# Fewer unread products ahead of the first real ones, and an earlier read of the last flag

## The chip, the cores and the metric

The kernel runs on one core of one Trainium2 chip. The metric is the device time of one execution in microseconds, as the median of several timed executions. Before the change it is 584.61 us (three executions, 584.51 to 585.43). A profiled execution is slower by what the profiler adds and is shown beside it.

## The reference

Two blocks follow one another. The first is a gated linear attention over 4 batches, 8 heads, 768 tokens and heads of 48; the second is a bilinear feed-forward over the 3072 resulting tokens with a model width of 384 and an inner width of 1536. All values are float32.

```python
def _attn_ref(q, k, v, f_logit):
    f = 1.0 / (1.0 + np.exp(-f_logit))
    state = np.zeros((B, H, D, D), dtype=np.float32)
    for t in range(S):
        state = f[:, :, t, :, None] * state + np.einsum('bhd,bhe->bhde', k[:, :, t], v[:, :, t])
        y[:, :, t] = np.einsum('bhd,bhde->bhe', q[:, :, t], state)
    return y

def _moe_ref(x, w_a, w_b, w_out):
    return (x @ w_a) * (x @ w_b) @ w_out
```

## The kernel before, in words

The program is one long straight line, with an order written by hand at the front, an order made by a planner behind it, and a branch at the end.

The attention is cut into 16 units: a unit is one batch, one half of the tokens (384) and four heads. For each unit the gates are turned into running products along the tokens; k is multiplied by the inverse products and q by the products, both on VectorE (line 374). After that the unit is plain matrix work on TensorE (PE): `turn` (line 455) transposes k, ScalarE copies it out (`turned`, line 462), `scores` (line 426) makes the 64 x 64 blocks of q times k, VectorE masks them (line 443), `gains` (line 506) makes each block's addition to the state, VectorE sums these (`carried`, lines 535 and 537), `within` (line 566) multiplies the masked scores by v and `across` (line 592) adds the part that comes from the state. ScalarE copies the unit's output from PSUM (`out_of_bank`, line 610) and DMAs store it into the tile `xT` (line 632), where the feed-forward reads it. The DMAs of the first two units are spread over the queues of SP, ScalarE and GpSimd, and all weight loads are issued on SP's queue, in program order between the other DMAs.

The feed-forward works on blocks of 384 tokens. Block 0 and 1 use plain products (`up`, line 676), the later blocks a scheme with fewer products and more sums (`up_triples`, line 803), and `down_thirds` (line 1010) does the same for the second matrix. The weights are converted in pieces on ScalarE, GpSimd and VectorE (lines 71 to 83, started by `begin` and finished by `end`).

At the front nothing of the feed-forward can run yet: the gates of units 0 and 1 must be turned into products, and the first weights loaded and converted. PE would stand idle. There the kernel issues matrix products whose result nobody reads, with `keep_up(n, width, rows)` (line 1195): the identity times some columns of the gate products, into a PSUM bank that is overwritten later. Before the change there are 17 of 128 columns ahead of `turn(0)`, 10 of 128 columns behind `gains(0)`, and 47 on 64 rows and 64 columns behind these, ahead of `turn(1)`; three more of 384 columns stand between the output of unit 1 and the first `up`, and stay. A float32 product is two matmul instructions on PE, each with its own weight load, so the profile counts it twice. Which engine does what is written down in program order, and each engine runs its own instructions in that order.

At the end the last block's `down_thirds(blk, ending)` makes, in this order, the products v1, u1, v2, r2, u2, v3, r3, u3, v4, t1, u4, v5, t2, u5, v6, each of four float32 products (eight matmul instructions). From them three row groups of the output are summed in the tile `w_ba`: row group 0 out of u3, t1, u4, v4, v5 and t2, group 1 out of u1, r2 and others, with its left half finished by v6 alone, and group 2 out of v1, v2, r3, u5 and others. The method assumes that the gates do not decay too far. A flag `bad` tells whether they did: VectorE sums what was noted on the way (`sum_held`), PE adds that over the partitions (line 1153), VectorE compares it (line 1154), and `read_bad` (line 1159) loads the flag into a register of every engine's sequencer. Then every engine branches (line 142): with the flag set, the whole output is computed again by another method; otherwise the last sums and stores run, which are kept in the list `ending`, and the program is over. In the input at hand the flag is not set.

Of the kernel before, what the change touches and what calls it, by code (L numbers as in the profile page):

```python
# [109 lines left out]
def kernel(  # L110
# [29 lines left out]
    with ExitStack() as pools:  # L140
        again, ending = by_quotients(pools, tc, q, k, f_logit, v, moe_w_a, moe_w_b, moe_w_out, out, ident, weights, bad, banks)
# [12 lines left out]
def by_quotients(ctx, tc, q, k, f_logit, v, moe_w_a, moe_w_b, moe_w_out, out, ident, weights, bad, ps_f):  # L154
    nc = tc.nc
    B, H, D, S = q.shape
    w_ba, w_out = weights
# [120 lines left out]
    def begin(n):  # L278

        while 2 * n > begun[0] < 2 * len(todo):  # L280
            i, second = divmod(begun[0], 2)
            dst, src, shape = todo[i]
            if not second:
                going.append(
                    from_double(
                        nc, dst, raws[i], shape[0], next(blocks), bits[i % len(bits)], some, whole, shape[0] == NKT
                    )
                    if src.dtype != FP32 else iter(())
                )
            next(going[i], None)  # L290
            begun[0] += 1
# [18 lines left out]
    PE, DVE, ACT, POOL, SP = range(5)  # L310
# [135 lines left out]
    def turn(u):  # L446

        kf = halves(sets[u % NSET]["k"])
        live.setdefault(u, {})["kT"] = sb1.tile([128, 2, NC, R + D], FP32, tag="kT", name="kT")
        ps = live[u]["turned"] = [ps_f[idle.pop(0)] for _ in range(2)] if u in FIRST else pair_of(away(u))  # L450
        used = ident[0:R + D, 0:R + D]
        for n in range(2):
            for c in range(NC):
                o = n * BLK + c * C
                nc.tensor.transpose(ps[n][:, c * (R + D):(c + 1) * (R + D)], kf[0:R + D, o:o + C], used)
# [37 lines left out]
    def gains(u, chunks=range(NC), halves=range(2)):  # L493

        _, half, _ = unit(u)
        t, kT = sets[u % NSET], live[u]["kT"]
        last = half == NH - 1
        ps = live[u]["turned"]
        for n in range(2):
            for c in chunks:  # L500
                for p in halves:
                    if last and c == NC - 1 and p == 1:
                        continue
                    for h in range(2):
                        r = slice(SUB * p, SUB * p + SUB)
                        nc.tensor.matmul(  # L506
                            ps[p][R * h:R * h + D, (n * NC + c) * D:(n * NC + c) * D + D],
                            lhsT=kT[r, n, c, R * h:R * h + D],
                            rhs=t["v"][r, n, c, h * D:h * D + D],
                            start=True,  # L510
                            stop=True,
                        )
        if chunks[0]:
            return
        st = sb2.tile([128, NJ - 1, 2, D], FP32, tag="st", name="st")
        before = live[u - NQ]["st"][NJ] if half else None
        live[u]["st"] = [before] + [st[:, j] for j in range(NJ - 1)]
        if not last:
            live[u]["st"].append(sb3.tile([128, 2, D], FP32, tag="st_end", name="st_end"))
# [135 lines left out]
    def on_pe(load, do, *args):  # L655
        beats[0] += 1
        return PE, load, 0, do, *args

    def on(engine, load, due, do, *args, copied=False):
        return engine + COPIED * copied, load, beats[0] + due if due else 1 << 30, do, *args  # L660
# [66 lines left out]
    HM = DM // 2  # L727
# [258 lines left out]
    def down_thirds(blk, ending=None):  # L986
# [11 lines left out]
        c = w_ba[:, 0, 0, 0:3 * BLK] if ending is not None else last[:, 3 * BLK:6 * BLK]  # L998
        c = c.rearrange("p (k i m) -> p k i m", k=NTG, i=2)
        places = last[:, 0:BLK], last[:, BLK:2 * BLK] if ending is None else w_ba[:, 0, 0, 3 * BLK:4 * BLK]  # L1000
        first, second = (x.rearrange("p (n m) -> p n m", n=2) for x in places)
        v, u, r, t = (ps_f[i][:, 0:HM] for i in free)
# [11 lines left out]
        def times(to, name, start=False):  # L1014
            for i in range(0, NJ3, 2):
                yield on_pe(BEAT, emit, to, left[name], more_of_w[name], start, i)

        def copy(due, to, ps):
            return on(ACT, 220, due, nc.scalar.copy, to, ps)
# [4 lines left out]
        def add(due, k, i, ps):  # L1024
            return on(DVE, 270, due, add_steps, c[:, k, i], c[:, k, i], ps, ALU.subtract if k == 1 else ALU.add)
# [41 lines left out]
        yield copy(5, c[:, 0, 1], u)  # L1067
        yield from times(v, "v4")
        yield copy(5, second[:, 1], v)
        yield from times(t, "t1", True)  # L1070
        yield copy(5, c[:, 0, 0], t)
        yield from times(u, "u4")
        yield add(5, 0, 0, u)
        if ending is not None:
            yield on(SP, 600, 0, read_bad)
        yield from times(v, "v5")
        yield copy(5, second[:, 0], v)
        yield from times(t, "t2")
        if ending is not None:
            yield from times(u, "u5")  # L1080
            yield from times(v, "v6")
            ending.extend((
                (add_steps, c[:, 0, 1], c[:, 0, 1], t), (add_steps, c[:, 0], c[:, 0], second), (store, 0),
                (store, 1, slice(1, 2)), (add_steps, c[:, 2, 0], u, c[:, 2, 0]), (store, 2),
                (write, c[:, 1, 0], v, -1), (store, 1, slice(0, 1)),
            ))
            return
# [84 lines left out]
    with tc.manual_schedule():  # L1172
# [17 lines left out]
        def keep_up(n, width=BLK, rows=128):  # L1190

            to = ps_f[idle[-1]]
            x = products_of_f[0][:, 0]
            for _ in range(n):
                nc.tensor.matmul(to[0:rows, 0:width], lhsT=ident[0:rows, 0:rows], rhs=x[0:rows, 0:width], start=True, stop=True)  # L1195

        def step(u, part, *which):
            for i in which:
                emit_all(parts[u][part][i:i + 1])
# [35 lines left out]
        step(0, 3, 1)  # L1235
        begin(0.5)
        begin(1)
        keep_up(17, 128)
        turn(0)
        turned(0)  # L1240
        scores(0)
        begin(1.5)
        begin(2)
        gains(0)
        keep_up(10, 128)
        step(1, 1, 0)
        keep_up(47, 64, 64)
        step(1, 1, 1)
        step(1, 2, 0)
        step(1, 1, 2)  # L1250
# [132 lines left out]
        main, beside, behind, ending, loaded_by, converted = [], {}, {}, [], {}, 0  # L1383
# [21 lines left out]
        for blk in range(NBLK):  # L1405
            if blk >= 2:
                beside[len(main)] = "x", blk
                main.extend(up_triples(blk))
                behind[blk] = len(main)
                ahead = 16  # L1410
            if blk == 1:
                parts = [
                    ("out", partial(down, two, place))
                    for two, place in (
                        (((0, 1), (0, 2)), outs), (((0, 0), (1, 0)), groups[:, NTG + 1]), (((1, 1), (1, 2)), outs)
                    )
                ]
            else:
                parts = [("thirds", partial(down_thirds, blk, ending if blk == NBLK - 1 else None))] if blk else ()
            for mark, part in parts:  # L1420
                beside.setdefault(len(main), mark)
                first, *steps = part()
                at = len(main) - ahead
                main.insert(at, first)
                beside = {n + (n > at): x for n, x in beside.items()}
                main.extend(steps)
                behind.setdefault("second" if "down" in behind else "down", len(main))
                ahead = 10
            if blk == 1:
                behind["halves"] = len(main)  # L1430
# [513 lines left out]
```

## Time and profile before

| | us |
|---|---|
| median of the timed executions | 584.61 |
| the profiled execution's own time | 586.35 |
| its span, from the first to the last instruction | 584.5 |
| PE busy | 565.9 (97%) |
| VectorE busy | 440.7 (75%) |
| ScalarE busy | 292.5 (50%) |
| GpSimd busy | 92.0 (16%) |
| mean granted clock of PE | 0.994 |

Times in the views are counted from the first instruction of the span. DVE is VectorE, ACT ScalarE, POOL GpSimd, SP SyncE, and PEld PE's weight load; a q behind an engine's name is its sequencer, which waits, branches, loads registers and issues DMAs. "issue" is time in which an engine waited for nothing that the profile shows. A line of the chain of waits gives start, duration and what; a line of the order of instructions gives start, duration, engine, line, operation, what is written and read, and how many instructions of that kind stand together, in brackets the idle time before. The DMA view names queues: q1 carries what the program issues, q8 and q14 the engines' own instructions.

### The profile page before, as it was taken

The page shows a single profiled execution, that of the slowest core. Times are in us where ns is not written, and L with a number is a line of the kernel's source. Part 1 is how long each engine was busy: PE and PEld are TensorE (multiplying, and loading weights), DVE is VectorE, ACT ScalarE, POOL GpSimd, SP SyncE. Part 2 cuts the span into 40 slices and gives each one's busy share as a digit, 9 for nine tenths or more (in the row PEclk, how much of TensorE's full clock was granted, in tenths as well). Part 3 has the DMA queues.
Part 4 walks back from the last instruction along what each step waited for, and adds up shares of the span by engine and source line. Part 5 has one row for each costly group of instructions (what it writes and reads, how often), then busy time and mean ns, then how long its engine had stood idle before and what let it go on. Part 6 is the DMA issues. An engine that isn't in the chain of part 4 may idle for free.

```text
span 584.5 us, 14158 instructions
## 1 busy us (share of the span) xinstructions
PE 565.9 (97%) x5842; PEld 510.1 (87%) x5842; DVE 440.7 (75%) x817; ACT 292.5 (50%) x562; POOL 92.0 (16%) x77
## 2 busy tenths in 40 slices
PE   5899999999999999999999999999999999999996
PEld 4765565656999999999999999999999999999995
DVE  6488936797999976977779686988779655946691
ACT  7459688833223655246561656346461545234521
POOL 4346546631010311010010101010000000000000
PEclk9999999999999999999999999999999999999998
DMA  8859669241436870430342223321440300010001
GB/s 192 209 152 328 192 175 297 99 78 37 88 82 131 131 137 3 102 66 5 79 106 44 65 62 67 78 65 25 49 100 2 66 21 6 17 40 1 2 0 49
DMA packets 46571, 50.33 MB, mean 86 GB/s; under 512 B 16592, under 2 KB 40320, under 8 KB 46496
## 3 DMA queue, kind: packets, MB, share of 16 engines
q1 hardware_dynamic: 42816, 45.48, 31.5%
q0 software_dynamic: 3552, 3.69, 4.3%
q8 instruction: 48, 0.79, 0.6%
q14 instruction: 27, 0.22, 0.1%
q10 hardware_dynamic: 128, 0.15, 0.1%
HBM read 33.23 MB, written 4.72 MB: 65 GB/s over the span
## 4 chain that ended last, share of the span: by engine, by line
PE 89%; DMA 4%; ACT 2%; DVE 2%; issue 1%; SPq 1%; DVEq 0%; ACTq 0%
PE ps_f L803 39%; PE ps_f L1010 20%; PE ps_f L676 13%; PE ps_f L896 7%; PE ps_f L1195 2%; PE ps_y L566 2%; PE ps_x L426 2%; DMA raw<-in_moe_w_b_dram 2%; PE ps_y L592 2%; PE ps_x L506 1%; DMA groups<-in_moe_w_a_dram 1%; ACT groups L1591 1%; DMA f_in<-in_f_logit_dram 1%; ACT k_in L610 1%; ACT sums L1591 0%
## 5 line engine op out<-in xcount | busy, mean ns | idle before, releaser
L1591 ACT COPY groups<-ps_f 128x384 f32<-128x384 f32 (+1 forms) x156 | 69.2, 444 | 112.0 <-PE ps_f L1010 44.7
L676 PE MATMUL ps_f<-xT,w_ba 128*128 128x384 f32 x288 | 96.7, 491 | 2.2 <-DMA xT<-groups 1.4
L676 PEld LDWEIGHTS ps_f<-xT,w_ba 128*128 128x128 f32 x288 | 53.4, 190 | 39.0 <-DMA xT<-groups 2.0
L1591 ACT COPY sums<-ps_f 128x384 f32<-128x384 f32 x120 | 57.5, 480 | 46.4 <-PE ps_f L803 33.6
L803 PE MATMUL ps_f<-xT,w_ba 128*128 128x192 f32 x384 | 79.0, 328 | 0.1
L803 PEld LDWEIGHTS ps_f<-xT,w_ba 128*128 128x128 f32 x384 | 64.4, 190 | 1.3 <-ACT groups L1591 0.7
L73 POOL TENSOR_SCALAR sums<-sums 128x768 f32<-128x768 f32 (+1 forms) x20 | 52.7, 2633 | 45.9 <-ACT sums L71 45.9
L803 PE MATMUL ps_f<-groups,w_ba 128*128 128x192 f32 x288 | 56.0, 329 | 0.0
L342 POOL TENSOR_SCALAR inv<-inv 128x768 f32<-128x768 f32 x13 | 12.6, 968 | 271.9 <-ACT inv L336 247.2
L803 PE MATMUL ps_f<-x_sums,raw 128*128 128x192 f32 x288 | 53.5, 330 | 0.3 <-DVE groups L795 0.3
L803 PEld LDWEIGHTS ps_f<-x_sums,raw 128*128 128x128 f32 x288 | 47.2, 190 | 2.4 <-ACT sums L1591 1.6
L803 PEld LDWEIGHTS ps_f<-groups,w_ba 128*128 128x128 f32 x288 | 47.8, 190 | 0.5
L795 DVE TENSOR_TENSOR groups<-groups 128x512 f32<-128x512 f32 (+2 forms) x52 | 42.4, 818 | 5.5 <-ACT groups L1591 3.5
L795 DVE TENSOR_TENSOR sums<-ps_f,sums 128x384 f32<-128x384 f32 x60 | 33.1, 553 | 15.5 <-PE ps_f L803 13.6
L795 DVE TENSOR_TENSOR sums<-sums,groups 128x768 f32<-128x768 f32 (+1 forms) x39 | 34.0, 873 | 13.9 <-ACT groups L1591 13.3
L795 DVE TENSOR_TENSOR groups<-ps_f,groups 128x384 f32<-128x384 f32 x60 | 33.0, 553 | 9.3 <-PE ps_f L803 7.6
L803 PE MATMUL ps_f<-xT,raw 128*128 128x192 f32 x192 | 39.5, 328 | 0.6 <-ACT groups L1591 0.6
L803 PE MATMUL ps_f<-x_sums,w_ba 128*128 128x192 f32 x192 | 39.2, 327 | 0.0
L1010 PE MATMUL ps_f<-spare,groups 128*128 128x192 f32 x192 | 35.2, 327 | 0.0
L803 PEld LDWEIGHTS ps_f<-xT,raw 128*128 128x128 f32 x192 | 32.3, 190 | 1.4 <-ACT groups L1591 1.2
L1010 PE MATMUL ps_f<-w_out,groups 128*128 128x192 f32 x192 | 33.2, 326 | 0.0
L803 PEld LDWEIGHTS ps_f<-x_sums,w_ba 128*128 128x128 f32 x192 | 32.5, 190 | 0.1
(198 smaller groups left out, 1006.1 us busy)
## 6 DMA issues: line engine op xcount, KB each, us to landing
k_in<-in_k_dram SPq DMA_DIRECT2D x32, 144.0 KB, 3.5
q_in<-in_q_dram SPq DMA_DIRECT2D x32, 144.0 KB, 4.2
v_in<-in_v_dram SPq DMA_DIRECT2D x16, 288.0 KB, 5.3
raw<-in_moe_w_out_dram SPq DMA_DIRECT2D x6, 768.0 KB, 7.3
f_in<-in_f_logit_dram SPq DMA_DIRECT2D x28, 144.0 KB, 3.2
out_dram<-groups SPq DMA_DIRECT2D x17, 192.0 KB, 1.9
raw<-in_moe_w_b_dram SPq DMA_DIRECT2D x4, 768.0 KB, 9.8
raw<-in_moe_w_a_dram SPq DMA_DIRECT2D x4, 768.0 KB, 11.0
```

The costliest lines, as they stand in the source:

```text
L73: nc.gpsimd.tensor_scalar(h, h, HI_MIN, HI_MAX, ALU.max, ALU.min)
L342: nc.gpsimd.tensor_scalar(inv, inv, EXP_K, 1.0, ALU.mult, ALU.add)
L426: nc.tensor.matmul(ps[h][SUB * p:SUB * p + SUB, o:o + SUB], lhsT=kf[r, tokens(n, c, p)], rhs=qf[r, tokens(n, c, p)], start=True, stop=True,)
L566: nc.tensor.matmul(ps[p][e:e + D, o:o + SUB], lhsT=t["v"][r, n, c, h * D:h * D + D], rhs=at[r, h, o:o + SUB], start=o == 0, stop=True, ski ...
L592: nc.tensor.matmul(ps[p][e:e + D, o:o + SUB], lhsT=st[j][r, n], rhs=qf[r, tokens(n, c, p)], start=False, stop=True, skip_group_check=True,)
L676: nc.tensor.matmul(ps[nm][:, 0:BLK], lhsT=w[:, kt, ft * 128:ft * 128 + 128], rhs=xT[blk][:, kt], start=kt == 0, stop=kt == NKT - 1,)
L795: nc.vector.tensor_tensor(to, x, y, op)
L803: nc.tensor.matmul(ps[:, g], lhsT=sums_of_w[name][:, g, 128 * j:128 * j + 128], rhs=sums_of_x[blk][name], start=start and g == 0, stop=Tru ...
L896: nc.tensor.matmul(to, lhsT=x[:, i], rhs=w[:, i], start=start and i == 0, stop=i == HFT - 1, skip_group_check=True,)
L1010: nc.tensor.matmul(to, lhsT=x[:, i], rhs=w[:, i], start=start and i == 0, stop=i == NJ3 - 1, skip_group_check=True)
L1195: nc.tensor.matmul(to[0:rows, 0:width], lhsT=ident[0:rows, 0:rows], rhs=x[0:rows, 0:width], start=True, stop=True)
L1591: do(*args)
```

## The change

At the front 11 and 7 products of 128 columns stand where 17 and 10 stood, and the 47 tiny ones are gone. In the last block the flag is read two products earlier, between v4 and t1 instead of between u4 and v5; u4 is not added by VectorE from PSUM but copied by ScalarE into a free place of `w_ba`, and the sum with it joins the list behind the branch. In that list the store of the right half of row group 1, which is complete by then, goes first, ahead of all sums.

```diff
         yield from times(v, "v4")
         yield copy(5, second[:, 1], v)
+        if ending is not None:
+            yield on(SP, 600, 0, read_bad)
         yield from times(t, "t1", True)
         yield copy(5, c[:, 0, 0], t)
         yield from times(u, "u4")
-        yield add(5, 0, 0, u)
         if ending is not None:
-            yield on(SP, 600, 0, read_bad)
+            u_before = w_ba[:, 0, 1, 0:HM]
+            yield copy(5, u_before, u)
+        else:
+            yield add(5, 0, 0, u)
         yield from times(v, "v5")
         yield copy(5, second[:, 0], v)
         yield from times(t, "t2")
...
             ending.extend((
+                (store, 1, slice(1, 2)), (add_steps, c[:, 0, 0], c[:, 0, 0], u_before),
                 (add_steps, c[:, 0, 1], c[:, 0, 1], t), (add_steps, c[:, 0], c[:, 0], second), (store, 0),
-                (store, 1, slice(1, 2)), (add_steps, c[:, 2, 0], u, c[:, 2, 0]), (store, 2),
+                (add_steps, c[:, 2, 0], u, c[:, 2, 0]), (store, 2),
                 (write, c[:, 1, 0], v, -1), (store, 1, slice(0, 1)),
             ))
...
-        keep_up(17, 128)
+        keep_up(11, 128)
         turn(0)
         turned(0)
         scores(0)
         begin(1.5)
         begin(2)
         gains(0)
-        keep_up(10, 128)
+        keep_up(7, 128)
         step(1, 1, 0)
-        keep_up(47, 64, 64)
         step(1, 1, 1)
```

## The prediction

> **What bounds the kernel now.** I read the page first: TensorE (PE) is busy 97% of the span, and in its chain of work PE has 89%. So time can only go where PE has nothing to do: in front of the first real work and behind the last. The chain of waits, in order of time, shows the front (start, us, what):
>
> ```profile
> 7.26 5.94 PE ps_f L1195 x34
> 13.20 0.58 PE ps_f L455 x6
> 13.78 0.86 PE ps_x L426 x48
> 14.63 0.54 PE ps_f L506 x48
> 15.18 6.36 PE ps_f L1195 x85
> 21.53 0.33 issue
> 21.87 1.85 PE ps_f L1195 x29
> 23.71 0.73 PE ps_f L455 x6
> 24.44 0.86 PE ps_y L426 x48
> 25.30 0.66 PE ps_x L566 x44
> 25.96 1.98 issue
> ```
>
> L1195 are the unread products: 34 + 85 + 29 = 148 records for 74 products, two each. They hold PE until 23.71, when unit 1 is turned. Two gaps are called "issue": no semaphore explains them. Between the two gaps lie 29 + 6 + 48 + 44 = 127 matmuls, each with its own weight load: 254 instructions. That is a block of instructions:
>
> ```profile
> PE 565.9 (97%) x5842; PEld 510.1 (87%) x5842; DVE 440.7 (75%) x817; ACT 292.5 (50%) x562; POOL 92.0 (16%) x77
> q8 instruction: 48, 0.79, 0.6%
> q8 instruction: 1, 0.02, 4.5%
> q8 instruction: 1, 0.02, 5.0%
> ```
>
> Queue 8 brings 48 packets in the span and PE has 2 x 5842 instructions, 243 a packet. The last two rows are from the DMA view of 19.0 to 20.5 and of 25.2 to 26.6: one packet ahead of the end of each gap. So PE stands because its next block of instructions is not there. [...] The stages (start:end length, then busy us and count of PE, weight load, VectorE, ScalarE, GpSimd; granted clock, DMA share, GB/s):
>
> ```profile
> 21.87:25.96 4.09, 4.09 (x127) 3.73 (x127) 0.59 (x1) 1.77 (x4) 0.07 (x1) 1.00 0.95 236
> 25.96:27.94 1.98, 0.00 (x0) 0.00 (x0) 0.36 (x1) 1.95 (x4) 1.98 (x1) 1.00 0.04 16
> 28.32:31.74 3.42, 3.42 (x121) 3.38 (x111) 1.74 (x7) 0.16 (x1) 1.17 (x2) 0.50 0.03 7
> ```
>
> The block that PE waits for from 25.96 was asked for, I infer, when PE crossed the border at 21.87: 6.07 us before 27.94, with the DMA engines at 0.95. After the gap the clock is granted at 0.50 for 3.42 us. What follows:
>
> ```profile
> 27.64 0.84 ACT L333 ACTIVATE f_in<-f_in 128x768 f32<-128x768 f32 x1
> 32.16 1.45 ACT L610 COPY groups<-ps_x 48x384 f32<-48x384 f32 x3 [3.68 <-PE ps_x L592]
> 33.63 1.45 ACT L610 COPY groups<-ps_y 48x384 f32<-48x384 f32 x3
> 36.63 4.14 PE L676 MATMUL ps_f<-xT,w_ba 128*128 128x384 f32 x12 [1.39 <-DMA xT<-groups]
> 30.16 1.87 PE L592 MATMUL ps_x<-q_in,st 48*48 48x64 f32 x37
> 31.87 0.89 PE L592 MATMUL ps_y<-q_in,st 48*48 48x64 f32 x32
> ```
>
> The outputs of units 0 and 1 leave PSUM (L610), go by DMA into x, and the first real matmul (L676) starts at 36.63. All weight loads behind it are issued after those stores on SP's queue. From there to the end the order of work is fixed and nothing goes by absolute time, so what 36.63 gains the end gains.
>
> **The front, step by step.** 17, 10 and 47 products become 11, 7 and none: 56 products, 112 matmul records and 112 weight loads less, 0.9 of a block. First, what each removed product hid:
>
> ```profile
> 10.47 0.96 DVE L374 TENSOR_TENSOR k_in<-k_in,inv 128x768 f32<-128x768 f32 x1
> 12.29 0.73 ACT L75 ACTIVATE spare<-raw,some 128x384 f16<-128x384 f32 x1
> 13.53 0.78 ACT L462 COPY kT<-ps_f 128x336 f32<-128x336 f32 x2 [0.51 <-PE ps_f L455]
> 16.82 0.96 DVE L374 TENSOR_TENSOR k_in<-k_in,spare 128x768 f32<-128x768 f32 x1
> 18.57 0.95 DVE L374 TENSOR_TENSOR q_in<-q_in,groups 128x768 f32<-128x768 f32 x1
> ```
>
> - 17 to 11: 34 records take 5.94 us, the first ones slower, so 22 end between 11.1 (at the mean) and 12.0; I take 11.7. The turn of unit 0 needs k (11.43): with its 0.58 it ends near 12.3, the scores with 0.86 near 13.2. The gains need the two copies behind ACT's L75 (13.02), so 13.85 instead of 14.46 (14.63 in the chain): 0.5 us, not 1.5.
> - 10 to 7, 47 to 0: PE is free at 16.0. The turn of unit 1 needs k at 17.78, the scores q at 19.52, then the first `within`: PE reaches it at 20.4, at 21.2 if its idle time has halved the clock.
> - The blocks. The 221 records before the gap at 21.53 are the same count afterwards, but other work: 22 + 6 + 48 + 48 + 14 + 6 + 48 = 192, so the border lies at the 29th of the 48 matmuls of `within` of unit 0. PE arrives there between 20.9 and 21.8; the block, asked for at most 0.5 us earlier than now, is there between 21.4 and 21.9. The next border, 127 later, is at the 20th of the 40 matmuls of `across` of unit 0 (20 of `within`, 32 gains, 48 of the next `within`, 8 gains before it). PE runs into it by about 24 and stands until the block is there: 6.07 us after 21.4 to 21.9, so 27.5 to 27.9. I take 27.7.
> - So the stall stays, even longer; but PE then stands at the 20th of `across`, which it passes now near 31.0 (37 of them from 30.16 to 31.87, half a clock). That is the gain.
> - From 27.7: PE stood for over 3 us, so I take the half clock. 20 more at (31.87 - 30.16)/37 = 46 ns: 28.7, so L610 of unit 0 starts at 28.75 instead of 32.16: 3.4 us. `across` of unit 1 takes 40 x 46 ns: 30.6, so L610 of unit 1, free of unit 0's copies by 30.2, starts near 30.8 instead of 33.63: 2.8 us. The loads queue on SP behind its stores, so 2.8 us counts. VectorE and ScalarE have their share of unit 2 done earlier, having been held by the same PE gap.
> - Bounds. Low: block at 27.94, half clock to the end of the three wide products (six records of 0.65 us instead of 0.33), which then end at 35.2 and hold the first real matmul there: 1.4 us. High: block at 27.4 and full clock (0.89/32, under 28 ns each): `across` ends at 28.0, L610 of unit 1 follows that of unit 0 at 29.4: 4.2 us. I take 2.8, since the row at 28.32 shows the half clock after a shorter gap.
>
> **The tail.** The last products, the flag `bad` and its reads (TENSOR_LOAD on every engine's sequencer), and the end:
>
> ```profile
> 570.62 0.14 DVE L1154 TENSOR_SCALAR bad<-ps_x 1x1 int32<-1x1 f32 x1
> 570.87 4.06 PE L1010 MATMUL ps_f<-w_out,groups 128*128 128x192 f32 x24
> 577.37 1.46 PE L1010 MATMUL ps_f<-groups 128*128 128x192 f32 x8
> L1159 PEldq TENSOR_LOAD <-bad x1: 493/493/493, 570.8 to 570.8; - x1
> L1159 DVEq TENSOR_LOAD <-bad x1: 537/537/537, 573.8 to 573.8; - x1
> 577.40 0.35 DVE L795 TENSOR_TENSOR w_ba<-w_ba,ps_f 128x192 f32<-128x192 f32 x1 [3.31 <-issue]
> 578.45 1.83 SPq L1029 DMA_DIRECT2D out_dram<-w_ba  x4
> 578.93 0.33 ACT L715 ACTIVATE w_ba<-ps_f 128x192 f32<-128x192 f32 x1 [3.64 <-PE ps_f L1010]
> out_dram<-w_ba SPq DMA_DIRECT2D x1, 192.0 KB, 3.6
> out_dram<-w_ba SPq DMA_DIRECT2D x1, 96.0 KB, 3.3
> q8 instruction: 1, 0.02, 5.4%
> ```
>
> - VectorE reads the flag at 573.8, behind its sum with u4, and its next instruction behind the branch starts 3.6 us later, at 577.40. With that sum moved behind the branch it reads at 570.8 and is through at 574.4. The sum of t2, over on PE at 576.2, then starts at 576.3 and store 0 goes about 1.1 us earlier (0.6 with PE's stall, next); the sum moved there (0.35 us) fits in before. The copy of u4 by ScalarE (0.32 us) stands in the place of nothing else there.
> - PE: its read now runs at 570.8, though 16 matmuls ahead of it in the program start only from 570.87: its sequencer runs that far ahead. Put 16 matmuls earlier, the read is reached long before `bad` (570.76), waits, and takes 0.49 us: t1 can be sent only at 571.3 instead of 570.87. With the restart 0.5 us, behind which all of PE's last 40 matmuls queue. Bounds: 0 if the read doesn't hold what follows, 0.6.
> - The last store waits for ScalarE's copy of v6 (579.26) and for three stores before it on SP (issued at 579.95, four in 1.83 us). One of them now goes out long before; so the last is issued 0.03 behind its copy: 579.8, 0.15 earlier, the PE stall included. The two last stores land 3.6 and 3.3 us after their issue (the DMA view of each one's issue), and between 580.2 and 581.8 a packet of instructions takes an engine's turn. With the other stores gone before it I take 0.4 off the last one's 3.3. Tail: 0.6 us gained, from a loss of 0.3 (PE's stall and nothing else) to a gain of 2.0 (the last store lands ahead of that packet, 1.4 us sooner still; no row shows which comes first).
>
> Sum: 2.8 + 0.6 = 3.4 us. The profiled execution took 586.35 with a span of 584.5; the sum is a difference, taken from the median of the timed runs, 584.61: 581.2.
>
> **The rivals.**
> - Block hidden: were blocks early for a PE that runs further ahead, `across` would end near 24 and L610 would wait for ScalarE alone, whose sigmoid of unit 2 (L333, 27.64 to 28.48 now, about 27.3 then) stands before it: 27.4 and 28.9 for 32.16 and 33.63, 4.8 us, time 579.2. Against it: two gaps in a row above. [...]
> - Late and cold: the low bound with a tail of 0.2, 583.0. It is also where one window of 3.42 us at half clock falls on the real matmuls (1.7 us lost).
> - No gain: two such windows on L676 cost 3.4 us: 584.6. Against it: PE is busy without break there, and at 31.87 one busy window had brought the clock back.
> - Slower: the products are there to keep the clock up, and without them PE stays at half clock through the first real products. A matmul of L676 costs 4.14/12 = 0.345 us, as much again at half clock; the gain of 3.4 is used up at 10 of them, slower by over 0.2% from 14. Two whole products (24) give 584.6 - 3.4 + 8.3 = 589.5. Speaking for it: PE now idles from 16.0 to 17.8, 18.4 to 19.5 and some 3.5 us before 27.7. [...]
>
> **How the numbers follow.** Forecast 0.64, block hidden 0.10, late and cold 0.14, no gain 0.08, slower 0.04. A measurement of this kernel tells 0.2%, 1.17 us, from no change: faster 0.64 + 0.10 + 0.14 = 0.88, same 0.08, slower 0.04. The range takes in the forecast, block hidden and late and cold with their bounds, 579.0 to 583.4, and leaves the other 0.12 outside.
>
> **What would show it.** Right: a gap "issue" of over 3 us in front of L592 of unit 0 that ends near 27.7; L610 near 28.8; the first L676 near 33.8; weight loads after it as much earlier; VectorE's first sum behind the branch near PE's t2; a gap of about half a microsecond on PE ahead of t1. Wrong: L676 starting as before, or at half clock; the gap gone; PE's gap at the flag over 1 us.

## The result and the profile after

The changed kernel takes 581.74 us in the median (six executions, 580.90 to 582.15), beside 585.54 for the kernel before on the same chip (584.51 to 586.17): a ratio of 0.9938, with a 95% interval of 0.9925 to 0.9950, or 2.9 to 4.4 us less. The profiled execution took 581.81 with a span of 579.8, 4.5 and 4.7 less than before.

First the page, then the chain of waits at the front (start, us, what):

```profile
PE 561.6 (97%) x5730; PEld 505.7 (87%) x5730; DVE 440.9 (76%) x817; ACT 292.5 (50%) x563; POOL 93.4 (16%) x77
q8 instruction: 47, 0.77, 0.5%
```

```profile
20.75 1.34 PE ps_x L566 x46
...
23.99 0.56 PE ps_x L592 x19
24.55 2.80 issue
27.35 0.78 PE ps_x L592 x14
...
29.80 0.34 PE ps_f L506 x4
...
34.10 3.87 PE ps_f L676 x12
```

PE has 112 matmuls and 112 weight loads fewer, and queue 8 brings one packet fewer. One long gap is left. It lies behind the first 19 or 20 matmuls of `across` of unit 0 and ends at 27.35. The order of instructions shows what follows it (the unread products stand on line 1200 now):

```profile
28.53 1.45 ACT L610 COPY groups<-ps_x 48x384 f32<-48x384 f32 x3 [1.76 <-PE ps_x L592]
30.00 1.45 ACT L610 COPY groups<-ps_y 48x384 f32<-48x384 f32 x3
30.00 3.15 SPq L632 DMA_DIRECT2D xT<-groups  x5
33.26 1.04 SPq L234 DMA_DIRECT2D k_in<-in_k_dram  x2
30.07 4.03 PE L1200 MATMUL ps_f<-groups,ident 128*128 128x384 f32 x6
33.94 4.04 PE L676 MATMUL ps_f<-xT,w_ba 128*128 128x384 f32 x12
```

The outputs of units 0 and 1 are copied 3.63 us earlier than before (32.16 and 33.63), and the loads that stand behind the stores on SP's queue go 3.6 earlier with them. The three wide products run at half clock (granted 0.50 until 33.80), 4.03 us for six, and the first real product starts at 33.94, 2.7 earlier than at 36.63. Yet some 30 us later PE is 4.2 us ahead. The order of instructions around that place, before and after:

```profile
52.43 8.23 PE L676 MATMUL ps_f<-xT,w_ba 128*128 128x384 f32 x24
62.86 4.46 PE L676 MATMUL ps_f<-xT,w_ba 128*128 128x384 f32 x12 [0.76 <-DVE w_ba L83]
```

```profile
49.63 8.01 PE L676 MATMUL ps_f<-xT,w_ba 128*128 128x384 f32 x24
59.00 4.14 PE L676 MATMUL ps_f<-xT,w_ba 128*128 128x384 f32 x12
```

Up to the first row of each fence the lead is 2.8 (52.43 and 49.63), that of the first real product. Then, before, PE waited 0.76 and a little more for weights that VectorE converts (line 83). Afterwards those are there in time and the same twelve products run in one piece, through at 63.14 (59.00 + 4.14) instead of 67.32 (62.86 + 4.46). The chain of waits of before goes back from here to a weight load of 9.54 us that landed at 58.09; but VectorE was busy for 4.00 us of the four from 56 to 60 and for 3.97 of the next four, so it isn't shown that this load held it. The tail of the changed kernel:

```profile
L1164 PEldq TENSOR_LOAD <-bad x1: 494/494/494, 566.6 to 566.6; - x1
566.44 0.14 DVE L1159 TENSOR_SCALAR bad<-ps_x 1x1 int32<-1x1 f32 x1
567.14 3.87 PEld L1010 LDWEIGHTS ps_f<-w_out,groups 128*128 128x128 f32 x24 [0.58 <-DVE bad L1159]
567.17 4.14 PE L1010 MATMUL ps_f<-w_out,groups 128*128 128x192 f32 x24 [0.31 <-issue]
570.47 0.36 DVE L795 TENSOR_TENSOR w_ba<-w_ba 128x192 f32<-128x192 f32 x1 [3.89 <-ACT w_ba L1595]
575.31 0.33 ACT L715 ACTIVATE w_ba<-ps_f 128x192 f32<-128x192 f32 x1 [3.64 <-PE ps_f L1010]
out_dram<-w_ba SPq DMA_DIRECT2D x1, 96.0 KB, 3.0
```

PE's sequencer waits for the flag and loads it, and the weight loads of t1 stand 0.58 for it. VectorE's first sum behind the branch now starts at 570.47, 4.8 ahead of ScalarE's last copy; before, it started at 577.40, 1.5 ahead of it. The last store (the DMA view of its issue, the last row) takes 3.0 from issue to landing instead of 3.3.

### The profile page after: what moved, and what is told of

It is laid out like the page before. It is cut to its first block, busy times and chain, and to the rows that moved or that the text cites. A ratio compares the mean times of both kernels' runs of the same rounds, so it can differ in the third digit from the quotient of the medians.

```text
span 579.8 us, 13936 instructions
## 1 busy us (share of the span) xinstructions
PE 561.6 (97%) x5730; PEld 505.7 (87%) x5730; DVE 440.9 (76%) x817; ACT 292.5 (50%) x563; POOL 93.4 (16%) x77
## 4 chain that ended last, share of the span: by engine, by line
PE 93%; DVE 3%; ACT 2%; issue 1%; DMA 1%; SPq 0%; DVEq 0%; ACTq 0%
PE ps_f L803 39%; PE ps_f L1010 20%; PE ps_f L676 16%; PE ps_f L896 7%; PE ps_y L566 2%; PE ps_y L592 2%; PE ps_x L426 2%; PE ps_x L506 1%; PE ps_f L1200 1%; DVE groups L346 1%; ACT groups L1595 1%; DMA f_in<-in_f_logit_dram 1%; ACT k_in L610 1%; ACT sums L1595 0%; PE ps_x L592 0%
## 5 line engine op out<-in xcount | busy, mean ns | idle before, releaser
L676 PE MATMUL ps_f<-xT,w_ba 128*128 128x384 f32 x288 | 96.1, 490 | 0.0
L676 PEld LDWEIGHTS ps_f<-xT,w_ba 128*128 128x128 f32 x288 | 53.9, 190 | 35.9 <-issue 0.5
```

The lines of the kernel that those rows point to most:

```text
L676: nc.tensor.matmul(ps[nm][:, 0:BLK], lhsT=w[:, kt, ft * 128:ft * 128 + 128], rhs=xT[blk][:, kt], start=kt == 0, stop=kt == NKT - 1,)
```

## The experiments

Each kernel ran beside the kernel before on the same chip; a ratio is to that, with its 95% interval. "Theory" is the one of the prediction: PE stands because its next block of instructions is not there, so the number of instructions says where and the DMA traffic says how long.

**Front alone.** The two edits of the front, the tail as before.

```diff
-        keep_up(17, 128)
+        keep_up(11, 128)
...
-        keep_up(10, 128)
+        keep_up(7, 128)
         step(1, 1, 0)
-        keep_up(47, 64, 64)
```

> The front of the changed kernel (11, 7 and no unread products) with the tail of the kernel before. Theory (the gain comes from the border of the third instruction block, which now falls into across of unit 0, and the tail adds about half a microsecond more): the trace shows the gap of about 2.8 us in front of the 20th matmul of across, ending near 27.4, the first matmul of up near 34, PE 4.0 to 4.3 us earlier than before from 66 on, no gap at the flag, and the slow landing of the last stores as before: 3.5 to 4.2 us faster than before in time. Rival (the tail carries the gain): under 2 us faster.

Measured: 581.66 beside 584.73, ratio 0.9945 (0.9927 to 0.9962), 2.2 to 4.3 us less: the whole gain, within what can be measured. From its chain:

```profile
24.70 1.07 PE ps_x L592 x19
25.77 1.48 issue
27.25 0.50 PE ps_x L592 x14
...
60.50 0.44 DVE w_ba L83
60.98 2.20 PE ps_f L676 x6
```

Here PE was slow from an earlier time on (the 48 matmuls of L426 ahead of `within` took 1.56 us, in the changed kernel 1.15) and reached the border 1.2 later than there (25.77 and 24.55), and the gap is shorter by as much: its end, 27.25 beside 27.35, did not move with the time at which PE got there. At 60.98 PE waits for the same converted weights as before at 65.12, 4.1 earlier. The first real product starts at 32.45, 1.5 ahead of the changed kernel's (behind this gap the first 14 matmuls took 0.50 us instead of 0.78), but with that wait PE is no further by 63 us: the twelve products end at 63.18 here and at 63.14 there.

**Tail alone.** The front as before, the tail of the change.

```diff
-        keep_up(11, 128)
+        keep_up(17, 128)
...
-        keep_up(7, 128)
+        keep_up(10, 128)
         step(1, 1, 0)
+        keep_up(47, 64, 64)
```

> The front of the kernel before (17, 10 and 47 unread products) with the tail of the changed kernel. Theory: PE loses 0.6 us ahead of t1, where its read of the flag waits for it, and the last stores, issued earlier, land 1.1 us sooner after PE's end than before: 0.2 to 0.8 us faster in time. Rival (the tail carries the gain): 2 us faster or more. Second rival (the stall at the flag costs more than the stores gain): 0.3 to 1 us slower.

Measured: 584.78 beside 584.73, ratio 1.0012 (0.9993 to 1.0031): no gain is seen. The interval goes from 0.4 us less to 1.8 more, so the 0.2 to 0.8 that I had expected is neither found nor wholly ruled out. Its table of waits near the end has the stall:

```profile
PEld ps_f L1010 <- DVE bad L1159: 0.6, 1, 0.6
```

**As many instructions as before.** The front of the change, with the removed products put back at 16 columns, so that PE has the count of before at a smaller cost each.

```diff
         keep_up(11, 128)
+        keep_up(6, 16)
...
         keep_up(7, 128)
+        keep_up(3, 16)
         step(1, 1, 0)
+        keep_up(47, 16, 64)
```

> The changed kernel with as many unread products as the kernel before, but 56 of them with 16 columns only (17 = 11 of 128 columns and 6 of 16; 10 = 7 of 128 and 3 of 16; 47 of 16 columns on 64 rows). PE's time for them is nearly that of the changed kernel, the number of instructions that of the kernel before. Theory (the number of instructions decides, since PE waits for blocks of them): the gaps fall where they fell before, one inside the tiny products until about 21.3 and one at the 45th matmul of within of unit 0 until 27.2 to 27.9; L610 of unit 0 starts near 31.5 and the first matmul of up near 36; against the kernel before 0.5 to 2 us faster, the tail included. Rival (the time on PE decides, the gap has another cause): like the changed kernel, 3.5 to 4 us faster, with its gap in across.

Measured: 585.68 beside 584.73, ratio 1.0024 (1.0003 to 1.0045). The gain is gone, and the 0.5 to 2 us less that I had expected did not come either: it is 0.2 to 2.6 us slower. In its chain the tiny products, 109 ns a record (3.17 us for 29; before it was 64, 1.85 for 29 of 64 columns), still fill PE, and L676 starts near where it did before:

```profile
21.27 3.17 PE ps_f L1200 x29
...
36.10 4.18 PE ps_f L676 x12
```

Behind them the 48 matmuls of L426 took 1.49 us instead of 0.86, so PE was slowed as well, and this kernel does not separate the count from the time; those with ten tiny products more and with wider ones, below, do. The gap that I had expected at the 45th of `within` isn't there: PE, slowed, reached it near 28.2 and went on (L566: 48 from 27.24, 1.02 us). The next one is, 0.91 us, ahead of the last matmuls of `across` of unit 0 (31.21), about 127 matmuls behind the 45th, as the count has it. Why the whole is slower than before, with a span 0.6 shorter in the profile, stays open.

**Flag's product ahead of r3.** The changed kernel with the flag computed 16 matmuls earlier.

```diff
+        if ending is not None:
+            yield on(PE, 100, 0, check_held)
         yield sum_of(15, s0, a32, a33)
         yield sum_of(15, s0, s0, a31, less)
         yield from times(r, "r3", True)
...
-        if ending is not None:
-            yield on(PE, 100, 0, check_held)
         yield from times(u, "u3")
```

> The changed kernel with the flag's product and comparison placed ahead of r3 instead of behind it, on PE and on VectorE; the read of the flag stays between v4 and t1. Theory (PE stands 0.6 us ahead of t1 because its read of the flag waits until 566.6 for the comparison): the comparison runs 2 us or more earlier, the gap ahead of t1 is gone or under 0.1 us, and PE's end comes 0.5 to 0.6 us earlier: 4.2 to 4.7 us faster than before, where the changed kernel is 3.8 faster. Rival (the load itself, 0.49 us, stops PE wherever it stands): the gap stays at 0.3 us or more.

Measured: 581.19 beside 584.73, ratio 0.9940 (0.9919 to 0.9961), not told apart from the changed kernel. The wait for `bad` is gone from PE's waits, though its read is as long as in the changed kernel (488 ns beside 494): what PE lost was the wait for the flag, not the load. The order of instructions of this kernel also has both borders, with a faster PE ahead of them (0.93 us for the 48 matmuls of L426, 1.15 in the changed kernel):

```profile
20.23 0.61 PE L566 MATMUL ps_x<-at,v_in 64*48 64x64 f32 x28
21.07 0.48 PE L566 MATMUL ps_x<-at,v_in 64*48 64x64 f32 x18 [0.23 <-issue]
27.09 0.50 PE L592 MATMUL ps_x<-q_in,st 48*48 48x64 f32 x14 [3.64 <-issue]
```

A gap ahead of the 29th of `within`, as counted in the prediction, and the next block at 27.09, 6.02 after 21.07. Before, it was 6.07; other kernels below have other values.

**Ten tiny products more.** Twenty records more in a place where PE waits for data anyway.

```diff
         keep_up(7, 128)
         step(1, 1, 0)
+        keep_up(10, 16, 64)
```

> The changed kernel with ten tiny unread products (16 of 128 columns, 64 rows) put back behind the seven: 20 matmul records more, about 0.5 us of PE time at a place where PE waits for q anyway. Theory (PE stands for its next block of instructions, so the count of records ahead of it says where): the gap in `across` of unit 0, which lies behind its 20th matmul in the changed kernel (ends 27.35), moves to ahead of its first one, and still ends at 27.1 to 27.7. Then all 40 matmuls come behind it, 20 x 46 ns = 0.9 us more: the copies of L610 0.9 us later than 28.53 and 30.00 and the time 0.5 to 0.9 us above the changed kernel's, about 582.4. Rival (the gap belongs to a place in the work or to data that is late there): the gap stays behind the 20th matmul and L610 at 28.5.

Measured: 582.52 beside 584.87, ratio 0.9959 (0.9944 to 0.9974); the median is where the theory had it, but the interval overlaps with the changed kernel's, so a price isn't resolved. The place is. From the chain:

```profile
24.45 0.31 PE ps_f L506 x8
24.76 2.05 issue
26.81 0.98 PE ps_x L592 x33
```

The gap has moved by twenty, to just behind the eight gains ahead of `across`. So nothing about `across` or its data holds PE there: the place went with the count. The price of the theory isn't in the trace, though, and the median agrees with it by luck. The gap ends 0.5 sooner than in the changed kernel, 0.3 below what I had expected, and the copies of L610, expected 0.9 later than 28.53 and 30.00, start at 28.0 and 29.5. The border before the gap lies twenty records earlier, but PE, which is slow here (1.28 us for the 48 of `within`; in the changed kernel the clock granted from 21 to 22 is 0.50), crosses it near 21.5 in both kernels, so an earlier request doesn't explain the earlier block. Its packet on queue 8 is listed at 24.1, when the bulk transfers run out; in the changed kernel both happen near 24.8.

**Wider unread products.** With the early flag; the same columns in 14 records instead of 36.

```diff
-        keep_up(11, 128)
+        keep_up(3)
+        keep_up(1, 256)
...
-        keep_up(7, 128)
+        keep_up(2)
+        keep_up(1, 128)
```

> The kernel with the flag's product ahead of r3 (581.19 before), and with fewer but wider unread products: three of 384 columns and one of 256 for the eleven of 128, two of 384 and one of 128 for the seven: the same columns, 14 records instead of 36. Theory (count): the border of the block moves 22 matmuls on, to the 2nd of the 40 of `across` of unit 1. `across` of unit 0 is then done ahead of the gap, near 24.6, its L610 near 25 to 28 (ScalarE has the sigmoid of unit 2 in between), and 38 matmuls of half clock (46 ns) behind a gap that ends at 27.2 give L610 of unit 1 at 29.0 instead of 30.0: 0.8 to 1.5 us below the kernel with the early flag, 579.7 to 580.4. Rival (what is left is held by something else, such as the half-clocked wide products or the weights): within 0.4 us of it, 580.8 to 581.6.

Measured: 580.04 beside 584.87, ratio 0.9918 (0.9901 to 0.9935), 3.8 to 5.8 us less: the fastest of the study in its median, though its interval overlaps with those of the changed kernel and of the kernel with the early flag. The border is where the count puts it, at the second or third matmul of `across` of unit 1:

```profile
25.59 0.26 PE ps_y L592 x2
25.85 1.33 issue
27.18 1.03 PE ps_y L592 x31
```

**No unread products there.** With the early flag, both `keep_up(11, 128)` and `keep_up(7, 128)` taken out.

```diff
-        keep_up(11, 128)
...
-        keep_up(7, 128)
```

> As the one before, with the early flag, but none of the eleven and seven unread products at all: 36 records fewer. Theory (count): the border lies at the 16th matmul of `across` of unit 1, 24 x 46 ns = 1.1 us are left behind the gap, L610 of unit 1 near 28.4 and the time 0.3 to 1.0 us below the kernel with wider products: 579.0 to 580.0. Rival (the products keep the clock up): without them PE works at half clock from unit 0's turn on, reaches the border and so its next request later, and the gap ends at 28 to 29: 581 to 583. Rival that was in the prediction as slower: half clock into the first real products, 585 or more.

Measured: 580.25 beside 584.87, ratio 0.9920 (0.9895 to 0.9945): as fast as the wider ones, 0.3 us above the range that the count alone gave. The border lies behind the 16th matmul of `across` of unit 1, as counted. The first rival has the slow PE in front right (1.56 us for the 48 matmuls of L426, 1.28 for those of `within`, beside 0.86 and 0.82 later on), and its gap, which ends 0.7 later than with wider products; but that costs no more than fewer records bring:

```profile
26.07 1.80 issue
27.87 0.51 PE ps_y L592 x18
```

That a later request makes the gap end later isn't shown. With wider products PE is as slow (1.56 and 1.28), and crosses the border before at about 22.4, here at about 22.6. What differs more is the packet, listed at 25.5 here and at 24.7 there, each time where the bulk transfers run out; why they last longer here stays open.

**No wide products.** The changed kernel without `keep_up(3)` ahead of the first `up`.

```diff
         y_of(1)
-        keep_up(3)
         begin(3)
```

> The changed kernel without the three wide unread products of 384 columns between `across` of unit 1 and the first real product. Theory (they run at half clock after the gap, end at 33.9 and hold the first L676 by up to 0.9 us): the first L676 starts near 33.0, and if the clock is back by then the time falls by 0.5 to 0.9: about 581.0. Rival (they are what brings the clock back: without them PE idles from 30.1 until x is there, and the first real products run at half clock for one window of 3.4 us or more): first L676 near 33.0, but six or more of them at 0.64 us, 1.7 us lost, 582.5 to 583.5.

Measured: 581.99 beside 585.07, ratio 0.9947 (0.9926 to 0.9969), not told apart from the changed kernel. From the chain:

```profile
32.83 6.76 PE ps_f L676 x12
39.59 0.58 PE ps_y L455 x6
```

The median lies between the two expectations. The rival was right about what these products do here: without them the first real products start 1.3 earlier, but the twelve take 6.76 instead of 3.87, and are through at 39.59 instead of 37.97, 1.6 later. The wide products hold the start by 1.3 and save 2.9.

**The last weight load later.** The changed kernel; the fourth weight load goes from SP at 16.89 to behind the stores of unit 1.

```diff
         across(0)
-        load_weights()
         y_of(0)
...
         y_of(1)
+        load_weights()
         keep_up(3)
```

> The changed kernel, with the fourth load of weights (issued at 16.89 on SP's queue, its bytes the last to move before the gap, until about 25.0) moved behind the outputs of units 0 and 1 (near 33). Theory A (the packet of instructions queues behind the bulk transfers on its DMA engine): the engines are free near 23.5, the packet that moves at 24.6 now moves about 1.2 us sooner, and the gap ends near 26, L610 of both units and the first real product up to 1.2 us earlier, if the later weights don't hold the products at 62 to 65. Theory B (the time from a block's request to its use doesn't depend on the load): the gap ends at 27.1 to 27.4 as before and the time is 581 to 583. The weights themselves come 16 us later; if they are waited for, PE shows it in the first 100 us as a wait on the conversion.

Measured: 583.81 beside 584.87, ratio 0.9977 (0.9961 to 0.9993). Theory A holds: with those bytes out of the way the instruction packet moves between 22 and 24 and the gap ends at 25.18, where the changed kernel's packet moves between 24 and 25 and its gap ends at 27.35. PE passed the 29th of `within` at about 20.9 (its 46 records of that line run from 20.40 to 21.29), so the block took about 4.3, where it took about 5.8 in the changed kernel (from 21.57 to 27.35). But the weights themselves were now late. The load took 5.26 us (second fence, the chain), and PE waited 1.83 us for what was converted from it (third fence, order of instructions). Its first twelve matmuls of L676, with a clock of 0.66 granted from 31 to 36, took 5.57 us instead of 4.04. Together this cost more than the 2.4 us by which the first real product came earlier (31.56):

```profile
25.18 0.50 PE L592 MATMUL ps_x<-q_in,st 48*48 48x64 f32 x14 [1.56 <-issue]
```

```profile
31.80 5.26 DMA raw<-in_moe_w_a_dram
```

```profile
42.53 0.91 PE L676 MATMUL ps_f<-xT,w_ba 128*128 128x384 f32 x2 [1.83 <-DVE w_ba L83]
```

**The same load by GpSimd, in between.** The kernel with wider products, the fourth load on GpSimd's queue ahead of the stores of unit 0.

```diff
         across(0)
-        load_weights()
+        load_weights(1, nc.gpsimd)
         y_of(0)
```

> The kernel with wider products and the early flag (580.04 before), with the fourth load of weights issued by GpSimd behind its work for unit 2 (near 28.3) instead of by SP at 16.89. It lands near 30.5, ahead of ScalarE's read of it near 32.4, so unlike the kernel that loaded it at 31.8 (block back at 25.18, but weights late and the time 583.81) nothing should wait for it. Theory A (the block's packet queues behind bulk transfers): the gap, now in `across` of unit 1 and ended at 27.18, ends at 25.0 to 25.8; L610 of unit 1 is then held by ScalarE alone, at 28.2 instead of 28.6, and the time falls by no more than 0.4: 579.4 to 580.2. If PE, done early, idles into the first real product at half clock, up to 581.5. Theory B (the block came early in the kernel before for another reason, such as its border lying elsewhere): the gap still ends near 27.2.

Measured: 584.11 beside 585.07, ratio 0.9976 (0.9962 to 0.9991). The block is there at 24.95, Theory A again, and the gap is down to 0.61 us. The time missed every expectation. The load landed 6.2 us after its issue, where I had allowed 2.2, and the stores of x, issued behind it, took 5.8 instead of the 2.2 they take in the kernel with wider products (third fence):

```profile
24.95 0.97 PE L592 MATMUL ps_y<-q_in,st 48*48 48x64 f32 x32 [0.61 <-issue]
35.15 1.65 PE L676 MATMUL ps_f<-xT,w_ba 128*128 128x384 f32 x2 [6.75 <-DMA xT<-groups]
```

```profile
raw<-in_moe_w_a_dram POOLq DMA_DIRECT2D x1, 768.0 KB, 6.2
xT<-groups SPq DMA_DIRECT2D x3, 72.0 KB, 5.8
```

```profile
xT<-groups SPq DMA_DIRECT2D x3, 72.0 KB, 2.2
```

PE then stood 6.75 us for x, and its first two records took 0.8 us each when it came. The wait for instructions had turned into a wait for data.

**Tail alone, with the early flag.** The kernel of the tail alone, with the flag's product moved as above.

```diff
+        if ending is not None:
+            yield on(PE, 100, 0, check_held)
         yield sum_of(15, s0, a32, a33)
...
-        if ending is not None:
-            yield on(PE, 100, 0, check_held)
         yield from times(u, "u3")
```

> The kernel before with the change's tail alone, and with the flag's product and compare ahead of r3, so that PE's read of the flag finds it written. The tail alone measured 1.0012 (0.9993 to 1.0031) of the time before. Theory (the tail's gain, which the prediction took as 0.6 net of a stall of 0.5, is eaten by PE's wait for the flag and nothing else): without the stall 0.5 to 0.7 us less, 584.0 to 584.4 beside 584.7, ratio near 0.999, and no gap at t1. Rival (the tail has nothing to give: what ends the run is the landing of the last store, which the packet of instructions on its engine sets): stall gone in the trace, last landing no earlier, and the time within 0.3 us of the kernel before.

Measured: 584.09 beside 585.07, ratio 0.9979 (0.9962 to 0.9995), 0.3 to 2.2 us less, and no stall at t1. From PE's last product to the end of the span it takes 5.0 us (578.72 to 583.7) instead of 5.7 (578.83 to 584.5), so the rival, by which the last store lands no earlier, isn't borne out either. So the tail has something to give once PE need not wait for the flag; the interval overlaps with that of the tail alone, so how much of the difference is the stall isn't shown by the times, only by the traces.

## Why the prediction was right, step by step

- **PE stands for blocks of instructions, and the count says where.** Right. The 29th of `within` shows as a border in the kernel with the early flag, the 20th of `across` in the changed kernel, and the border moved by 20 records one way and by 22 and 36 the other, as counted. That the count sets the place was tested by moving it; that what PE waits for is its next block of instructions is inferred, from the 127 matmuls between two borders and from the packet of queue 8 ahead of the end of each gap. The gap of 2.80 us was there, and the rival "block hidden" falls with it.
- **The block arrives 6.07 after the border before, at 27.7.** The time is right, but by luck. It was 27.35, and 27.25 and 27.09 in the two other kernels with this front. But the step that gave it, a fixed 6.07 from border to block, doesn't hold. From the border as counted, with PE's times, it was about 5.8 in the changed kernel (28 of the 46 records from 20.75 on are over near 21.57), 5.3 with the front alone, 4.8 with wider products and 4.3 with the late load. What the kernels have in common is the other end: the packet on queue 8 is listed when the bulk transfers run out, and PE goes on 2.4 to 2.9 us later. The transfers ended at nearly the same time before (25.4) and after (24.8), and so the 6.07 fitted.
- **Half clock behind the gap, L610 of unit 0 at 28.75, of unit 1 at 30.8.** The first is right (28.53). The second was mis-sized: I had the 60 matmuls behind the gap end at 30.6, at 46 ns each from 27.7. They run from 27.35 to 29.80, 41 ns each, so `across` of unit 1 was done when ScalarE had finished with unit 0, and its copy follows straight at 30.00. The loads gain 3.6, not 2.8.
- **First real product near 33.8, and what it gains the end gains.** The start was close (33.94), partly by luck: x was there earlier than I had it, but the half-clocked wide products, which I had in the low bound, held PE. With the front alone, where PE was faster behind the gap (0.50 us for the first 14 matmuls, 0.78 here), it is 32.45. The lead of 2.7 was carried, as forecast, to 52 us. The second half of the step failed in the traces: from 36.63 to the end the order is fixed, but it isn't free of waits. Before, PE waited for converted weights from 62.1 on; the changed kernel doesn't wait there and is 4.2 ahead behind that place, and the front alone, with 1.5 more of a lead, waits and is 4.1 ahead. That wait isn't the same in every execution: the two kernels with the front of before and the new tail are through the same twelve products at 66.88 and 66.51 instead of 67.32. So up to 0.8 of the 4.2 belongs to the one execution that was profiled. In the times the front alone gave 3.2 (2.2 to 4.3), where 2.8 was predicted.
- **The tail.** As a trace it came out piece by piece: PE's stall 0.58 for 0.5, VectorE's sums far ahead of ScalarE's last copy, the last store landing 3.0 behind its issue, 0.3 sooner for 0.4. From PE's last product to the end of the span it takes 4.6 us (575.22 to 579.8) instead of 5.7 (578.83 to 584.5): 1.1 gained and 0.58 lost, 0.5 in all. (The span of the tail alone is 0.5 shorter too, 584.0, but PE was 0.4 ahead in it at the products near 67 us, where the tail has no part.) In the times the tail alone gave between 0.4 less and 1.8 more, so 0.6 was at least 0.2 too much for that kernel; the profile's half microsecond is below what the times tell apart.
- **The rivals.** "Late and cold" came true in one part, half clock to the end of the wide products (granted 0.50 from 26.97 to 33.80), without its time, since by 63 us those cost nothing. "Slower" shows where the wide products are taken away: twelve matmuls of L676 take 6.76 us there instead of 3.87, by my estimate nine of them at half clock (2.89 more, at 0.32, which is 3.87/12, for each). That is the place where I saw it, but the products that stayed kept it away. "No gain" lies outside the interval.

The sum, 3.4, lies between the 2.9 and 4.4 of the interval. Its two terms seem to err in opposite ways, the front a little too small and the tail too large, and that nearly cancels; the times are too rough to size either error. The profile's 4.5 is above the interval: the profiled execution of before is 0.8 above the median of the six, that of the changed kernel 0.1, and the executions of the kernel before lie up to 1.7 us apart here and up to 4.8 in another comparison.

## What to carry to other kernels

Where an engine stands and nothing in the program explains it, count its instructions between gaps: here twenty records of cheap filler moved the gap by twenty records, and filler that covers the same columns in 14 records instead of 36 did no worse (0.9918 of the time before, beside 0.9940). Then ask what shares the DMA engines with what the engine waits for, and what else needs those bytes: both tries to clear the way here lost more on late weights or late x than they won (0.9977 beside 0.9938 of the changed kernel, 0.9976 beside 0.9918 of the kernel with wider products). And before a lead at the first real product is carried to the end, look for the next wait on the way, here one for converted weights, and ask whether it keeps, eats or adds to that lead, and whether it is the same in every execution.

## What the runs showed of the hardware

**Behind a window busy for 3.03 us of 3.41 the clock was still 0.50, and in one busy for 2.03 of 3.42 it stayed at 1.00.** The half clock behind the gap lasted 3.42 us before (28.32 to 31.74) and twice that after (26.97 to 33.80). So I cut both traces into windows of 3.41 us from these edges, here of the changed kernel and, in the second fence, of the kernel before (start:end length, busy us and count of PE, weight load, VectorE, ScalarE, GpSimd; granted clock, DMA share, GB/s):

```profile
26.97:30.38 3.41, 3.03 (x69) 2.94 (x70) 3.27 (x8) 1.80 (x4) 1.47 (x2) 0.50 0.02 5
30.38:33.80 3.42, 3.42 (x6) 1.87 (x6) 3.31 (x6) 1.98 (x4) 2.43 (x4) 0.50 0.50 142
```

```profile
35.15:38.57 3.42, 2.03 (x7) 1.17 (x7) 3.21 (x7) 2.08 (x3) 1.35 (x4) 1.00 0.69 190
```

After a window with PE busy 3.03 of 3.41 the next one, busy throughout, was still at 0.50; behind that one, from 33.80 to 37.20, it was 1.00. Before, in a window busy for only 2.03 of 3.42 it was 1.00, and in the next one too (38.57 to 42.00). So the half clock lasted two windows, 6.83 us, in the changed kernel where I had counted on one. What sets its end is not shown.

**With a bulk load out of the way the gap ended 4.3 us behind the border before it instead of 5.8.** From one border, as counted, to the first instruction behind the next one it took 4.8 to 6.1 us with that load issued at 16.89, and 4.3 and about 3.7 with it issued later. Queue 1 and queue 8 from 24 to 25 us of the changed kernel, then queue 1 from 25 to 26 (packets, MB, share of 16 engines):

```profile
q1 hardware_dynamic: 151, 0.28, 88.0%
q8 instruction: 1, 0.02, 6.8%
q1 hardware_dynamic: 19, 0.03, 8.8%
```

The packet, which takes about 1.1 us of one engine (6.8% of sixteen), is listed at 24.8, just as the bulk transfers run out, and PE goes on at 27.35. In the other kernels it is the same: listed at 25.4 and on at 27.94 before, 24.1 and 26.81 with ten tiny products more, 25.5 and 27.87 with no unread products there, 22.3 and 25.18 with the late load. That the time goes with the load's bytes was tested by moving them; how the packet comes to wait for them isn't shown.

**PE's read of the flag held the weight loads behind it for 0.58 us where the flag was still to come.** The read takes 0.49 us (494 ns in the changed kernel). With the flag written early it takes as much (488 ns, from 563.8), and PE's waits have no entry for `bad`.
